# Products into one set of columns, ACT stores straight from the bank, and Pool on every second subtraction: one stage of a mixture-of-experts kernel on one core

## The chip, the core and the metric

One NeuronCore of a Trainium2 chip. TensorE (PE) multiplies into the eight banks of PSUM, VectorE (DVE) and ScalarE (ACT) read PSUM and SBUF, GpSimd (POOL) reads and writes SBUF here, SyncE (SP) issues the DMAs. The metric is the device time of one execution in microseconds (us); lower is better.

## What is computed

```python
X = np.fft.fft(np.fft.fft(x, axis=1), axis=2).real   # x: (8, 3072, 256)
x = X.reshape(24576, 256)
# eight groups of 3072 rows in the kernel: soft routing of rows to 32 slots and back
logits = x @ phi
slot_out = experts(softmax(logits, axis=0).T @ x)     # two small matmuls per expert
y = softmax(logits, axis=1) @ slot_out
# second mixture: three matmuls, a maximum, one matmul
h = np.maximum(np.maximum(y @ w1, y @ w2), y @ w3)
out = h @ w_out                                       # (24576, 768) @ (768, 256)
```

The softmax of the second line is over all rows of the input, so everything up to `slot_out` ends before any row of `out` can begin. That splits the kernel into two phases. The change is in the second.

## The kernel before

The first phase ends at about 207.7 us of the profiled execution. The second one (from `phase2`, L1095) makes the output. The slots are folded into the weights ahead of it, so that only a 64-row operand `ct` (the softmax over slots, split into a high and a low half) is multiplied: `gst` holds what takes `ct` to the hidden layer, `w_hl` the last weights.

The work is cut into 48 **blocks** of 512 columns (`blocks`, `NK` = 48), six to a group `b` of the input: `q` = 0, 1, 2, and two halves `h` of each `q`. The first group that is done is the last one of the input. A block has six **steps**, one for each 128 rows `f` of the hidden layer; `n` = 6k + f numbers the steps through. In step n each engine is given, in this order:

- PE: two matmuls of 512 columns, L983 and L984 (`pmm`), into two banks; there are two banks of either kind, so L984 of step n waits until DVE has read that of step n-2.
- ACT: `relu` of the first bank (L989, to `t`), then `high` (L999): the rounded copy `hi` of the hidden tile of step n-1.
- DVE: `low` (L1004): `lo` = h - hi of step n-2; then a piece of the next group's softmax; then `top` (L994): the maximum of the second bank and `t`.
- PE: the products of an earlier block with the last weights. For each f and each 128 columns j: `hi` times [w_hi, w_lo], 512 columns in one instruction (L1014), for f = 0 one of 256 columns with `ct` (L1018), then `lo` times w_hi, 256 columns (L1021). Four accumulators `o` of one bank each hold j = 0 to 3. One block has 24 x (512 + 256) + 4 x 256 = 19,456 columns of this kind and 6 x 1024 of the first.

Each engine works its instructions off in that order. For blocks 0 to 2 the products of index i = 6k + f stand `behind[i]` = 3 to 6 steps behind, for all four j at once (`omm_f`). From step 24 on (`ahead`) they stand in the order j, f: 6, 11 and 4 x 13 pieces in steps 24 to 29, then 76 pieces in every six steps, which is one block. In that order the piece of f = 5, j = 0 of block m is the last one of step 6(m+1)+1, and its `lo` is subtracted in that same step.

When an accumulator is full, `fin` makes the output of it: the sum stands in two halves, hi x w_hi + lo x w_hi in columns 0 to 255 and hi x w_lo in 256 to 511. ACT copies the bank to SBUF (L1040, `ab`), and Pool adds the halves into `osb` (L1043). For q = 0 and 2 this is one add on 128 partitions, for q = 1 two adds on 64, since the halves of the partitions go to different rows. In the last block ACT copies one half and DVE adds the other from the bank. When `osb` is full, SP stores it: one DMA (L1054), or one and eight small ones (L1061, L1063).

The softmax of the next group (`softmax2`) begins with a DMA of its logits on SP (L596, `tmp`) in steps 12, 36, 72 and so on, and its pieces follow one to a step on DVE, the first of them three steps later: L609 twice, L612 twice, L617 twice, L620, L623 twice, L627 twice, then eight steps of two transposes each (L634). Pool is given five of the subtractions L1004 (`pool_low`: steps 13, 15, 18, 20 and 22).

Of the kernel before, what the change touches and what calls it, by code (L numbers as in the profile page):

```python
# [7 lines left out]
F32 = mybir.dt.float32  # L8
# [4 lines left out]
ALU = mybir.AluOpType  # L13
# [140 lines left out]
def kernel(ctx: ExitStack, tc: tile.TileContext, x, phi, w1, w2, u1, u2, u3, wo,  # L154
                        t_f, t_ft, t_s2, t_s2t, t_cm, t_inv, t_id, out):
    nc = tc.nc
    NB = x.shape[0]
    NP, LAST = NB // 2, NB - 1
    mm, act, dve = nc.tensor.matmul, nc.scalar.activation, nc.vector
    COPY, RELU, EXP = ACTF.Copy, ACTF.Relu, ACTF.Exp  # L160
# [44 lines left out]
    def dma(cost, out, in_, r=(), w=(), behind=()):  # L205
        def go():
            o = out() if callable(out) else out
            nc.sync.dma_start(out=o, in_=in_)
        return add("SP", cost, go, r, w, behind=behind)
# [380 lines left out]
    ct_t = {}  # L590
# [90 lines left out]
    def table_f(g, behind):  # L681
        lo, hi = GR[g]
        return dma(182 * (hi - lo), f_sb[:, lo:hi], t_f[:, lo:hi], w=[f"f{g}"], behind=behind)

    load_x(0, 0)
    k = table_f(0, [xa_at[0, 0]])
    k = dma(182, phi_sb, phi.rearrange("(h p) s -> p h s", p=128), w=["phi"], behind=[k])
    k = dma(273, s2_sb, t_s2, w=["s2"], behind=[k])
    load_x(0, 1, [k])
    k = table_f(1, [xa_at[0, 1]])  # L690
    load_x(0, 2, [k])
    k = table_f(2, [xa_at[0, 2]])
    k = dma(1456, cm_sb, t_cm, w=["cm"], behind=[k])
    k = dma(182, ident, t_id, w=["id"], behind=[k])
# [3 lines left out]
    k = dma(273, s2t_sb, t_s2t, w=["s2t"], behind=[xa_at[1, 1]])  # L698
    dma(2367, ft_sb, t_ft, w=["ft"], behind=[xa_at[1, 2]])
    add("DVE", 500, consts, r=["id"], w=["rep"])  # L700
    for b in range(NB + 2):
# [32 lines left out]
        if b == 7:  # L734
# [22 lines left out]
            for i in range(2):  # L757
                for h in range(2):
                    add("POOL", 1820, lambda i=i, h=h: nc.gpsimd.tensor_tensor(out=u12[:, i, h], in0=u12[:, i, h], in1=u3_sb[:, h], op=ALU.subtract),
                        r=["u30", "u31", "u32"] + [f"u{1 + i}{t}" for t in range(3)], w=[f"d{i}{h}"])  # L760
# [123 lines left out]
    w_hl = wg[:, 0:3072].rearrange("p (c f) -> p c f", c=6)  # L884
    w_hi, w_lo = w_hl[:, :, 0:256], w_hl[:, :, 256:512]
    gst = wg[:, 3072:4864]
# [41 lines left out]
    for a in range(2):  # L928
        for h in range(2):
            for k in range(2 + a):  # L930
                for i in range(4):
                    n = (112, 80)[a] if k < 2 else 64
# [3 lines left out]
                       start=(h == 0 and k == 0), stop=(h == 1 and k == 1 + a))  # L936
        o = sm[a][:, 0:224]
# [4 lines left out]
    for a in range(2):  # L942
        n = (112, 80)[a]
        for j in range(2):
            o = sm[4 + 2 * a + j][:, 0:448].rearrange("p (i c) -> p i c", i=2)
# [3 lines left out]
            c = 448 * a + 2 * n * j  # L949
# [14 lines left out]
    dp3 = ctx.enter_context(tc.tile_pool(name="dp3", bufs=3, reuse_waits="tile"))  # L964
# [10 lines left out]
    NK = len(blocks)  # L975
# [32 lines left out]

    def products(k, f, j, o):

        b, q, h = blocks[k]
        hi, lo = hl[k, f]
        c = slice(128 * j, 128 * j + 128)
        mm(out=o, lhsT=hi[:, c], rhs=w_hl[:, f], start=(f == 0), stop=False)  # L1014
        yield
        yield
        if f == 0:
            mm(out=o[:, 0:256], lhsT=ct_t[b][:, q, 512 * h + 128 * j:512 * h + 128 * j + 128], rhs=gst[:, 1536:1792],  # L1018
               start=False, stop=False)
            yield  # L1020
        mm(out=o[:, 0:256], lhsT=lo[:, c], rhs=w_hi[:, f], start=False, stop=(f == 5))  # L1021
        yield

    def omm(k):

        for j in range(4):
            o = ps_o.tile([128, 512], F32, tag="o", name="o")
            for f in range(6):
                yield from products(k, f, j, o)
            late.append(lambda o=o, j=j: fin(k, 4 * blocks[k][2] + j, o))  # L1030

    def fin(k, i, o):

        b, q, h = blocks[k]
        if i == 0:
            o_sb[b, q] = dp3.tile([128, 8, 256], F32, tag="osb", name="osb")
        osb = o_sb[b, q]
        ab = dp3.tile([128, 512], F32, tag="ab", name="ab")
        last = k == NK - 1
        act(out=ab[:, 256 * last:512], in_=o[:, 256 * last:512], func=COPY)  # L1040
        for r, e in ((slice(0, (128, 64, 0)[q]), i), (slice((128, 64, 0)[q], 128), 7 - i)):
            if r.start < r.stop:
                (dve if last else nc.gpsimd).tensor_tensor(out=osb[r, e], in0=(o if last else ab)[r, 0:256],  # L1043
                                                           in1=ab[r, 256:512], op=ALU.add)
        if k >= NK - 2 and (last or i == 3):

            j = i if last else 0
            o_k = out[b * 3072:b * 3072 + 2048].rearrange("(k g j) d -> k g j d", g=16, j=8)[:, 0:8, j:i + 1]
            nc.sync.dma_start(out=o_k.rearrange("k g j d -> k g (j d)"), in_=osb[:, j:i + 1].rearrange("p j d -> p (j d)"))
        if i < 7 or last:  # L1050
            return
        o_k = out[b * 3072:(b + 1) * 3072].rearrange("(k r) d -> k r d", r=128)
        def plus(p0, k0, n):
            nc.sync.dma_start(  # L1054
                out=o_k[k0:k0 + n, 0:64].rearrange("k (g j) d -> k g (j d)", j=8),
                in_=osb[p0:p0 + 8 * n].rearrange("p j d -> p (j d)"))
        def minus(p0, k0, n):

            blk_ = o_k[k0:k0 + n]
            v = blk_[:, 64:128].rearrange("k (g j) d -> k g j d", j=8)[:, ::-1]  # L1060
            nc.sync.dma_start(out=v[:, :, 1:8], in_=osb[p0:p0 + 8 * n, 0:7])  # L1061
            for g in range(8):
                nc.sync.dma_start(out=blk_[:, 128 - 8 * g if g else 64], in_=osb[p0 + g:p0 + 8 * n:8, 7])  # L1063
        if q == 0:
            plus(0, 0, 16)
        elif q == 1:
            plus(0, 16, 8)
            minus(64, 0, 8)
        else:
            minus(0, 8, 16)  # L1070

    def omm_f(k, f):

        if f == 0:
            for j in range(4):
                o4[j] = ps_o.tile([128, 512], F32, tag="o", name="o")
        if k < len(behind) // 6 - 1 or f < 3:
            parts = [(f, j) for j in range(4)]
        else:

            parts = [(3 + i % 3, i // 3) for i in range(4 * f - 12, 4 * f - 8)]
        for f, j in parts:
            for _ in products(k, f, j, o4[j]):
                pass
            if f == 5:
                fin(k, 4 * blocks[k][2] + j, o4[j])
# [1 line left out]
    o4 = [None] * 4  # L1088
    late = []

    pool_low = (13, 15, 18, 20, 22)
    ahead = [6, 11, 13] + [13] * 3 + [13, 13, 13, 13, 12, 12] * NK
    behind = (3,) * 6 + (4,) * 3 + (5,) * 3 + (6,) * 6

# [123 lines left out]
```

## Time and profile before

| | |
|---|---|
| three runs | 783.50, 783.26, 777.71 us (median 783.26) |
| the profiled execution | 782.51 us, of which 780.7 us from the first to the last instruction |
| first phase, to the first L983 | 207.7 us |
| second phase, to the last matmul | 207.7 to 775.8 us |
| after the last matmul | 4.9 us: ACT copy, DVE add, DMA |

The two numbers of the profiled execution differ by 1.8 us, which lie outside its first and last instruction. "Busy" is the share of time in which an instruction of the engine was under way. Matmuls overlap: a row gives one of 512 columns as lasting 0.39 us, though the next one starts 0.23 us after it. So what PE loses is read from the starts, not from the busy time.

### The profile page before, as it was taken

The numbers are of one execution on the slowest core, as the hardware profiler recorded it, in microseconds if no ns is written. First come the engines' busy times: TensorE is split into PE (matmuls) and PEld (weight loads), VectorE is DVE, ScalarE is ACT, GpSimd is POOL, SyncE is SP. The second block draws the span as 40 slices with busy tenths as digits, with TensorE's granted clock in tenths as the row PEclk, the third lists the DMA queues.
The fourth block names the chain that finished last, engine by engine and source line by source line (L and its number), as shares of the span: only waits on it lengthen the run. The fifth ranks groups of instructions, "written<-read, shape, count | busy, mean of one in ns | idle before, by whom it ended". The sixth has DMA issues, their size and how long they took to land.

```text
span 780.7 us, 14128 instructions
## 1 busy us (share of the span) xinstructions
PE 742.5 (95%) x5324; PEld 613.2 (79%) x5324; DVE 570.9 (73%) x925; ACT 520.3 (67%) x974; POOL 302.8 (39%) x322
## 2 busy tenths in 40 slices
PE   5989898978999999999999999999999999999997
PEld 4557676675687778888888888888888888888886
DVE  2577575548579979769867976896698679766663
ACT  2356454434378677778777877877787777777773
POOL 4044543433028522533352344335333522533521
PEclk9999989999999999999999999999999999999999
DMA  9987877698402414322502251242225114312113
GB/s 347 407 316 275 286 235 249 202 291 276 97 1 55 111 46 96 94 74 54 133 10 69 56 134 52 62 98 55 75 55 135 30 45 95 95 55 55 29 36 99
DMA packets 37220, 97.26 MB, mean 125 GB/s; under 512 B 6048, under 2 KB 16672, under 8 KB 35744
## 3 DMA queue, kind: packets, MB, share of 16 engines
q1 hardware_dynamic: 33696, 83.78, 36.6%
q0 software_dynamic: 3456, 12.58, 4.5%
q8 instruction: 42, 0.69, 0.4%
q14 instruction: 26, 0.21, 0.1%
HBM read 55.44 MB, written 28.31 MB: 107 GB/s over the span
## 4 chain that ended last, share of the span: by engine, by line
PE 76%; DVE 9%; DMA 6%; ACT 3%; SPq 3%; issue 2%; POOL 1%; DVEq 0%; ACTq 0%; POOLq 0%
PE o L1014 30%; PE o L1021 16%; PE p L984 8%; PE p L983 7%; PE ap L318 4%; DMA xb<-in_x_dram,rev_sb 4%; PE o L1018 3%; SPq L1063 2%; PE zp L339 2%; PE vp L491 1%; DVE xf L266 1%; PE ap L474 1%; DVE h L994 1%; DVE d L461 1%; PE sm L902 1%
## 5 line engine op out<-in xcount | busy, mean ns | idle before, releaser
L1014 PE MATMUL o<-wg,hi 128*128 128x512 f32 x1152 | 424.3, 395 | 0.0
L1043 POOL TENSOR_TENSOR osb<-ab 64x256 f32<-64x256 f32 (+1 forms) x252 | 217.8, 865 | 353.0 <-ACT ab L1040 332.1
L1021 PE MATMUL o<-wg,lo 128*128 128x256 f32 x1152 | 323.3, 281 | 1.1 <-DVE lo L1004 1.0
L994 DVE TENSOR_TENSOR h<-p,t 128x512 f32<-128x512 f32 x288 | 196.8, 684 | 101.7 <-ACT t L989 100.9
L1014 PEld LDWEIGHTS o<-wg,hi 128*128 128x128 f32 x1152 | 216.1, 188 | 42.5
L989 ACT ACTIVATE t<-p 128x512 f32<-128x512 f32 x288 | 171.7, 597 | 99.9 <-PE p L983 99.5
L1021 PEld LDWEIGHTS o<-wg,lo 128*128 128x128 f32 x1152 | 216.8, 188 | 20.5 <-DVE lo L1004 3.5
L999 ACT ACTIVATE hi<-h 128x512 fp32r<-128x512 f32 x288 | 180.4, 626 | 32.0 <-DVE h L994 31.6
L1004 DVE TENSOR_TENSOR lo<-h,hi 128x512 fp32r<-128x512 f32 x283 | 200.3, 708 | 0.3 <-ACT hi L999 0.2
L984 PE MATMUL p<-ct,wg 128*128 128x512 f32 x288 | 115.1, 400 | 2.2 <-DVE h L994 2.1
L1040 ACT ACTIVATE ab<-o 128x512 f32<-128x512 f32 (+1 forms) x192 | 111.6, 584 | 7.0 <-PE o L1021 7.0
L983 PE MATMUL p<-ct,wg 128*128 128x512 f32 x288 | 113.9, 396 | 0.0
L318 PE MATMUL ap<-ff_sb,xf 128*128 128x128 f32 x416 | 58.0, 295 | 13.7 <-DVE xf L266 7.8
L318 PEld LDWEIGHTS ap<-ff_sb,xf 128*128 128x128 f32 x416 | 53.5, 206 | 17.6 <-DVE xf L266 8.4
L984 PEld LDWEIGHTS p<-ct,wg 128*128 128x128 f32 x288 | 54.2, 188 | 11.4 <-DVE h L994 7.7
L983 PEld LDWEIGHTS p<-ct,wg 128*128 128x128 f32 x288 | 54.2, 188 | 8.0 <-ACT t L989 0.4
L1018 PE MATMUL o<-wg,ct 128*128 128x256 f32 x192 | 53.6, 279 | 0.0
L324 ACT ACTIVATE a_sb<-ap 128x512 f32<-128x512 f32 (+1 forms) x56 | 31.0, 571 | 33.2 <-PE ap L318 33.1
L1018 PEld LDWEIGHTS o<-wg,ct 128*128 128x128 f32 x192 | 36.2, 188 | 4.1
L634 DVE STREAM_TRANSPOSE tmp<-tmp 96x256 f32<-96x256 f32 x56 | 30.5, 619 | 0.0
L339 PE MATMUL zp<-a_sb,pj_sb 128*32 128x512 f32 (+1 forms) x256 | 26.5, 546 | 3.4 <-ACT a_sb L324 3.0
L233 POOL DMA_INDIRECT xb<-in_x_dram,rev_sb x24 | 24.2, 1008 | 13.0 <-DVE xf L266 8.0
(163 smaller groups left out, 555.0 us busy)
## 6 DMA issues: line engine op xcount, KB each, us to landing
wu<-in_moe_w_dram SPq DMA_DIRECT2D x32, 512.0 KB
ct<-tmp SPq DMA_DIRECT2D x84, 128.0 KB
xf<-in_x_dram SPq DMA_DIRECT2D x16, 512.0 KB
out_dram<-osb SPq DMA_DIRECT2D x7, 1024.0 KB
out_dram<-osb SPq DMA_DIRECT2D x8, 896.0 KB
xf<-in_x_dram SPq DMA_DIRECT2D x8, 640.0 KB
raw<-in_moe_w_dram SPq DMA_DIRECT2D x9, 512.0 KB
out_dram<-osb SPq DMA_DIRECT2D x9, 512.0 KB
```

The lines of the kernel that those rows point to most:

```text
L318: mm(out=ap[:, c, j], lhsT=x_t[b][:, 2 * i + j, 128 * c:128 * c + 128], rhs=f_sb[:, 2 * i + j])
L983: mm(out=p1, lhsT=gst[:, 128 * f:128 * f + 128], rhs=ct)
L984: mm(out=p2, lhsT=gst[:, 768 + 128 * f:768 + 128 * f + 128], rhs=ct)
L989: act(out=t1, in_=p1, func=RELU)
L994: dve.tensor_tensor(out=h32, in0=p2, in1=t1, op=ALU.max)
L999: act(out=hi, in_=h32, func=COPY)
L1004: (nc.gpsimd if n in pool_low else dve).tensor_tensor(out=lo, in0=h32, in1=hi.bitcast(F32), op=ALU.subtract)
L1014: mm(out=o, lhsT=hi[:, c], rhs=w_hl[:, f], start=(f == 0), stop=False)
L1018: mm(out=o[:, 0:256], lhsT=ct_t[b][:, q, 512 * h + 128 * j:512 * h + 128 * j + 128], rhs=gst[:, 1536:1792], start=False, stop=False)
L1021: mm(out=o[:, 0:256], lhsT=lo[:, c], rhs=w_hi[:, f], start=False, stop=(f == 5))
L1040: act(out=ab[:, 256 * last:512], in_=o[:, 256 * last:512], func=COPY)
L1043: (dve if last else nc.gpsimd).tensor_tensor(out=osb[r, e], in0=(o if last else ab)[r, 0:256], in1=ab[r, 256:512], op=ALU.add)
```

## The change

For blocks 0 to 7 and block 47 (`whole`) the 512-column matmul becomes two of 256 columns, with w_hi and with w_lo, into the same 256 columns of the bank. The finished sum then stands there complete. `fin` stores it to `osb` with ACT straight from the bank, one instruction of 128 partitions or two of 64; in the last block ACT and DVE take turns (j = 0, 2 and 1, 3). No `ab` and no Pool add remain in these nine blocks. The subtractions L1004 of all odd steps from 7 to 47 (21 instead of 5) go to Pool. Blocks 8 to 46 are as before.

```diff
     def products(k, f, j, o):
...
-        mm(out=o, lhsT=hi[:, c], rhs=w_hl[:, f], start=(f == 0), stop=False)
-        yield
-        yield
+        u = o[:, 0:256]
+        if whole(k):
+            mm(out=u, lhsT=hi[:, c], rhs=w_hi[:, f], start=(f == 0), stop=False)
+            yield
+            mm(out=u, lhsT=hi[:, c], rhs=w_lo[:, f], start=False, stop=False)
+            yield
+        else:
+            mm(out=o, lhsT=hi[:, c], rhs=w_hl[:, f], start=(f == 0), stop=False)
+            yield
+            yield
...
+    def whole(k):
+        return k < 8 or k == NK - 1
...
-        ab = dp3.tile([128, 512], F32, tag="ab", name="ab")
         last = k == NK - 1
-        act(out=ab[:, 256 * last:512], in_=o[:, 256 * last:512], func=COPY)
-        for r, e in ((slice(0, (128, 64, 0)[q]), i), (slice((128, 64, 0)[q], 128), 7 - i)):
-            if r.start < r.stop:
-                (dve if last else nc.gpsimd).tensor_tensor(out=osb[r, e], in0=(o if last else ab)[r, 0:256],
-                                                           in1=ab[r, 256:512], op=ALU.add)
+        parts = [(r, e) for r, e in ((slice(0, (128, 64, 0)[q]), i), (slice((128, 64, 0)[q], 128), 7 - i))
+                 if r.start < r.stop]
+        if whole(k):
+            for r, e in parts:
+                if last and i % 2:
+                    dve.tensor_copy(out=osb[r, e], in_=o[r, 0:256])
+                else:
+                    act(out=osb[r, e], in_=o[r, 0:256], func=COPY)
+        else:
+            ab = dp3.tile([128, 512], F32, tag="ab", name="ab")
+            act(out=ab, in_=o, func=COPY)
+            for r, e in parts:
+                nc.gpsimd.tensor_tensor(out=osb[r, e], in0=ab[r, 0:256], in1=ab[r, 256:512], op=ALU.add)
...
-    pool_low = (13, 15, 18, 20, 22)
+    pool_low = [n for n in range(7, 48) if n % 2]
```

How the order moves, at three places. On **POOL**, from the end of the first phase on (`u_110` is a weight of that phase; `osb` the output tile, `h_` with a number the hidden tile of one step), before:

```order
L759 TENSOR_TENSOR u_110<-u_110,u3o 128x768 x2
L1043 TENSOR_TENSOR osb<-ab 128x256 x4
L1004 TENSOR_TENSOR lo<-h_2383,hi 128x512
L1004 TENSOR_TENSOR lo<-h_2427,hi 128x512
L1043 TENSOR_TENSOR osb<-ab 128x256 x4
L1004 TENSOR_TENSOR lo<-h_2483,hi 128x512
L1004 TENSOR_TENSOR lo<-h_2531,hi 128x512
L1043 TENSOR_TENSOR osb<-ab 64x256 x2
L1004 TENSOR_TENSOR lo<-h_2582,hi 128x512
L1043 TENSOR_TENSOR osb<-ab 64x256 x14
L1043 TENSOR_TENSOR osb<-ab 128x256 x16
```

and now, from the ninth subtraction to the first add:

```order
L1004 TENSOR_TENSOR lo<-h_2648,hi 128x512
L1004 TENSOR_TENSOR lo<-h_2704,hi 128x512
L1004 TENSOR_TENSOR lo<-h_2754,hi 128x512
L1004 TENSOR_TENSOR lo<-h_2809,hi 128x512
L1004 TENSOR_TENSOR lo<-h_2873,hi 128x512
L1004 TENSOR_TENSOR lo<-h_2945,hi 128x512
L1004 TENSOR_TENSOR lo<-h_2998,hi 128x512
L1004 TENSOR_TENSOR lo<-h_3049,hi 128x512
L1004 TENSOR_TENSOR lo<-h_3106,hi 128x512
L1004 TENSOR_TENSOR lo<-h_3161,hi 128x512
L1004 TENSOR_TENSOR lo<-h_3214,hi 128x512
L1062 TENSOR_TENSOR osb<-ab 64x256 x16
```

The 40 adds of blocks 0 to 7 are gone, and Pool has 21 subtractions with nothing between them, before the first add of block 8 (L1062).

On **DVE**, steps 24 to 27, where the softmax pieces L627 and L634 of the next group stand (`tmp`, `p_` and `t_` are its tile, a bank and a `relu` tile), before:

```order
L627 TENSOR_TENSOR tmp<-tmp 96x512
L994 TENSOR_TENSOR h_2686<-p_2675,t_2678 128x512
L1004 TENSOR_TENSOR lo<-h_2656,hi 128x512
L627 TENSOR_TENSOR tmp<-tmp 96x512
L994 TENSOR_TENSOR h_2704<-p_2694,t_2697 128x512
L1004 TENSOR_TENSOR lo<-h_2686,hi 128x512
L634 STREAM_TRANSPOSE tmp<-tmp 96x256 x2
L994 TENSOR_TENSOR h_2726<-p_2715,t_2718 128x512
L1004 TENSOR_TENSOR lo<-h_2704,hi 128x512
L634 STREAM_TRANSPOSE tmp<-tmp 96x256 x2
```

and now:

```order
L627 TENSOR_TENSOR tmp<-tmp 96x512
L994 TENSOR_TENSOR h_2704<-p_2693,t_2696 128x512
L627 TENSOR_TENSOR tmp<-tmp 96x512
L994 TENSOR_TENSOR h_2734<-p_2723,t_2726 128x512
L1004 TENSOR_TENSOR lo<-h_2704,hi 128x512
L634 STREAM_TRANSPOSE tmp<-tmp 96x256 x2
L994 TENSOR_TENSOR h_2754<-p_2744,t_2747 128x512
L634 STREAM_TRANSPOSE tmp<-tmp 96x256 x2
L994 TENSOR_TENSOR h_2809<-p_2796,t_2799 128x512
L1004 TENSOR_TENSOR lo<-h_2779,hi 128x512
```

Each second L1004 has left this engine's row.

On **DVE**, the end of the program, before:

```order
L1004 TENSOR_TENSOR lo<-h_9289,hi 128x512
L994 TENSOR_TENSOR h_9334<-p_9325,t_9328 128x512
L1004 TENSOR_TENSOR lo<-h_9314,hi 128x512
L1004 TENSOR_TENSOR lo<-h_9334,hi 128x512
L1043 TENSOR_TENSOR osb<-o,ab 128x256 x4
```

and now:

```order
L1004 TENSOR_TENSOR lo<-h_9417,hi 128x512
L994 TENSOR_TENSOR h_9462<-p_9453,t_9456 128x512
L1004 TENSOR_TENSOR lo<-h_9442,hi 128x512
L1004 TENSOR_TENSOR lo<-h_9462,hi 128x512
L1055 COPY osb<-o 128x256 x2
```

Four adds that each need a copy of ACT first become two copies from the bank; the other two tiles are ACT's. On PE, 216 matmuls with their weight loads are added (24 in each of nine blocks); the number of columns is the same.

## Rows read from the trace of the kernel before

**Rows 1.** Windows: length, busy us of PE, PEld, DVE, ACT, POOL (instructions), clock, DMA.

```profile
207.67:226.59 18.92, 18.70 (x98) 15.08 (x97) 14.07 (x24) 14.62 (x30) 2.93 (x4) 1.00 0.00 0
226.59:247.48 20.89, 20.46 (x110) 17.24 (x109) 19.29 (x30) 17.72 (x34) 12.68 (x11) 1.00 0.20 51
247.48:321.33 73.85, 71.81 (x381) 58.93 (x380) 64.96 (x105) 54.45 (x102) 33.77 (x35) 1.00 0.38 92
532.14:555.44 23.30, 23.30 (x129) 20.10 (x128) 15.63 (x25) 17.32 (x32) 11.04 (x15) 1.00 0.12 33
```

**Rows 2.** Timeline of PE: start, duration, instruction [idle before, releaser], steps 25 and 41.

```profile
248.64 0.40 PE L983 MATMUL p<-ct,wg 128*128 128x512 f32 x1
249.68 0.50 PE L984 MATMUL p<-ct,wg 128*128 128x512 f32 x1 [0.64 <-DVE h L994]
...
282.60 0.39 PE L983 MATMUL p<-ct,wg 128*128 128x512 f32 x1
283.62 0.50 PE L984 MATMUL p<-ct,wg 128*128 128x512 f32 x1 [0.63 <-DVE h L994]
```

**Rows 3.** Timeline of PE and of its weight loads, where 256-column or shorter matmuls follow each other.

```profile
401.79 0.27 PE L1018 MATMUL o<-wg,ct 128*128 128x256 f32 x1
401.90 0.28 PE L1021 MATMUL o<-wg,lo 128*128 128x256 f32 x1
402.02 0.40 PE L1014 MATMUL o<-wg,hi 128*128 128x512 f32 x1
...
205.90 1.64 PEld L948 LDWEIGHTS sm<-gt,pick 128*128 128x128 f32 x14 [0.21 <-DVE gt L939]
```

**Rows 4.** Timeline of DVE, three neighbouring instructions of the transposing steps.

```profile
253.64 0.68 DVE L994 TENSOR_TENSOR h<-p,t 128x512 f32<-128x512 f32 x1
254.24 0.68 DVE L1004 TENSOR_TENSOR lo<-h,hi 128x512 fp32r<-128x512 f32 x1
254.84 1.11 DVE L634 STREAM_TRANSPOSE tmp<-tmp 96x256 f32<-96x256 f32 x2
255.80 0.67 DVE L994 TENSOR_TENSOR h<-p,t 128x512 f32<-128x512 f32 x1
```

**Rows 5.** Timeline of POOL and DVE: a subtraction alone, one beside a softmax piece.

```profile
228.22 1.29 POOL L1004 TENSOR_TENSOR lo<-h,hi 128x512 fp32r<-128x512 f32 x1 [3.17 <-ACT hi L999]
...
246.85 1.63 POOL L1004 TENSOR_TENSOR lo<-h,hi 128x512 fp32r<-128x512 f32 x1
...
247.24 1.78 DVE L623 TENSOR_TENSOR tmp<-tmp,sm__2460 96x512 f32<-96x512 f32 x1
```

**Rows 6.** Groups of DVE, 226 to 312 us.

```profile
L623 DVE TENSOR_TENSOR tmp<-tmp,sm__3071 96x512 f32<-96x512 f32 x2 | 1.4, 678 | 0.0
```

**Rows 7.** Groups of ACT, 207 to 312 us and the last 16 us.

```profile
L1040 ACT ACTIVATE ab<-o 128x512 f32<-128x512 f32 x30 | 17.1, 590 | 0.0
...
L1040 ACT ACTIVATE ab<-o 128x256 f32<-128x256 f32 x4 | 1.5, 385 | 7.0 <-PE o L1021 7.0
```

**Rows 8.** Timelines of ACT, POOL, SP's queue and DVE, around the load for steps 39 on.

```profile
265.11 0.60 ACT L1040 ACTIVATE ab<-o 128x512 f32<-128x512 f32 x1
...
264.29 4.31 POOL L1043 TENSOR_TENSOR osb<-ab 64x256 f32<-64x256 f32 x4 [2.18 <-ACT ab L1040]
...
269.33 9.40 SPq L1063 DMA_DIRECT2D out_dram<-osb  x8
...
282.28 0.68 DVE L609 TENSOR_REDUCE mx<-tmp 96x16 f32<-96x512 f32 x1 [3.08 <-DMA tmp<-l_dram]
```

**Rows 9.** Timelines of ACT and PE, steps 36 and 37.

```profile
273.76 0.62 ACT L999 ACTIVATE hi<-h 128x512 fp32r<-128x512 f32 x1
...
276.68 0.28 PE L1021 MATMUL o<-wg,lo 128*128 128x256 f32 x1
```

**Rows 10.** Timeline of the last 5 us.

```profile
775.86 0.38 ACT L1040 ACTIVATE ab<-o 128x256 f32<-128x256 f32 x1 [1.75 <-PE o L1021]
776.28 0.42 DVE L1043 TENSOR_TENSOR osb<-o,ab 128x256 f32<-128x256 f32 x1 [1.72 <-ACT ab L1040]
```

More of the change, by code (lines that the diff above doesn't have):

```diff
@@ L1013, in products @@
         c = slice(128 * j, 128 * j + 128)
-        mm(out=o, lhsT=hi[:, c], rhs=w_hl[:, f], start=(f == 0), stop=False)
-        yield
-        yield
+        u = o[:, 0:256]
[8 more added lines that the diff above has]
+            yield
         if f == 0:
-            mm(out=o[:, 0:256], lhsT=ct_t[b][:, q, 512 * h + 128 * j:512 * h + 128 * j + 128], rhs=gst[:, 1536:1792],
+            mm(out=u, lhsT=ct_t[b][:, q, 512 * h + 128 * j:512 * h + 128 * j + 128], rhs=gst[:, 1536:1792],
                start=False, stop=False)
             yield
-        mm(out=o[:, 0:256], lhsT=lo[:, c], rhs=w_hi[:, f], start=False, stop=(f == 5))
+        mm(out=u, lhsT=lo[:, c], rhs=w_hi[:, f], start=False, stop=(f == 5))
         yield
+    def whole(k):
+        return k < 8 or k == NK - 1
     def omm(k):
```

## The prediction

> **What bounds the kernel now.** I read three views, in this order. First the windows of the second phase [rows 1]. The reader is to see its last row first: two regular blocks, 23.30 us, in which PE is busy for all 23.30 and DVE for 15.63. There PE is the bound, and as these two blocks have 2 x 25,600 = 51,200 columns, a column costs 0.455 ns. With that price the rows above it can be weighed. Steps 0 to 11 hold 12 x 1024 columns of L983 and L984 and eight of the products' indices, 26,624 columns: 38,912 in all, 17.7 us, and they last 18.92. Steps 12 to 23 hold 44,032, 20.0 us, and last 20.89. Steps 24 to 59 hold 36 x 1024 + 6 x 19,456 columns less the seven pieces (1,792 columns) by which the first of those blocks starts slower: 151,808, 69.1 us, and last 73.85. So PE loses 1.2, 0.85 and 4.75 us there, 6.8 us in all, and hardly anything afterwards in a block as those of the last row. This is the whole that a better balance in the first ten blocks can give back.
>
> Then the timeline of PE, for whom it waits [rows 2]. L983 and L984 should start 0.233 us apart (512 x 0.455). In step 25 they are 1.04 apart, in step 41 1.02, and both times the releaser is DVE's L994. DVE is the late engine; it was busy for 19.29 of 20.89 and for 64.96 of 73.85 us [rows 1].
>
> Last, why DVE is late. There are three reasons. (a) In the transposing steps its own queue is longer than a step: L994 and L1004 start 0.60 us apart, as do L1004 and the transposes, and two transposes take 0.96, so 2.16 us a step [rows 4] against 11.65 / 6 = 1.94. (b) It is stretched by Pool: a softmax piece L623 lasts 0.68 us alone [rows 6] and 1.78 beside a subtraction on Pool, which itself goes from 1.29 to 1.63 [rows 5]. (c) In steps 39 and 40 it stands still for 3.08 us for the logits of the next softmax, whose load waits on SP behind the stores of a tile (eight of them fill 9.40 us of its queue), and these behind Pool's adds [rows 8].
>
> **The change part by part.** *Two matmuls of 256 columns for one of 512* (216 more on PE, with as many weight loads). Where 256-column matmuls with different weights follow each other they start 0.11 and 0.12 us apart [rows 3], and two of 0.1165 (256 x 0.455) are one of 0.233. Three and more in a row are new. The nearest row is the one of 14 weight loads back to back, in 1.64 us to the end of the last one [rows 3]: 1.64 / 14 = 0.117 at most from one to the next, and less by what the last one's own duration takes of it. So a weight load hides under a matmul of 256 columns. I take nothing; the bounds are 0 and 216 x 0.01 = 2.2 us, 0.01 being the difference between the two distances in rows 3. That all three write the same columns is no new thing either: L1018 and L1021 do so in these rows. The Trainium skill (TensorE: Matmul & The Clock Gate, Back-to-back issue gap) speaks against the split, as it gives each matmul some 2.5 ns on top of its columns; by it the sum would be 216 x 2.5 ns = 0.5 us worse, an estimate from that page. The rows, at 0.01 us, can neither show nor exclude such a step.
>
> *Pool's 40 adds of blocks 0 to 7 go, 16 more subtractions come* (21 instead of 5). Pool is no bound on either side: 21 x 1.29 to 1.63 us [rows 5] is 27 to 34 us in 41 steps of 1.94. On DVE the 16 are worth 0.60 us each [rows 4], 9.6 us, where they were on its path: in steps 24 to 33 two steps now hold 2 x (0.60 + 0.96) + 0.60 = 3.7 us against 3.9. The queue no longer grows, where it grew by 0.2 us in each. With L627 in steps 24 and 25 the reason (b) remains, one subtraction of Pool beside them instead of a row of adds. PE's loss in blocks 4 and 5, most of the 4.75, should fall to some 0.6.
>
> *The stores to SBUF by ACT.* A copy of 512 columns is 0.590 us and one of 256 is 0.385 [rows 7]. The blocks with q = 0 and 2 (0, 1, 4 to 7) save 4 x 0.205 = 0.8 us of ACT each. Blocks 2 and 3 (q = 1) need two of 64 partitions in place of one copy; no such row is there, and the nearest is the one of 128 partitions with as many columns, 0.385, so 4 x 0.18 = 0.7 us more in each. ACT is busy for 17.72 of 20.89 us in steps 12 to 23 [rows 1], so this fits, though with little to spare. In the row behind these stores stand the next `relu` and `high`, for which DVE waits. I take 0; bounds 0 to 1.5 us.
>
> *What the earlier output does to SP.* The last copy of block 3 ends at 265.7 us, and the adds behind it at 268.6 [rows 8]. With ACT storing twice 0.385 from 265.1 on, the tile is complete at about 265.9. SP's stores and the load behind them move up by 2 us or a little more, and so does the landing at 282.28. DVE, which stood there for 3.08 us, then still waits for about 1 us, and L994 of step 41 is no longer late: its 0.8 us, and the lateness it leaves to the next steps, go. I put that at 1.4 us of the 4.75.
>
> *The subtraction of f = 5 on Pool.* In steps 31, 37 and 43 it is needed in the same step. `hi` is ready at 274.38 and PE uses the first of it at 276.68 [rows 9], 2.3 us later; Pool needs 1.29 to 1.63. It is in time, with 0.7 us or more to spare.
>
> *The last block.* A copy and an add of 0.42 end at 776.70, 0.84 us after the bank was ready [rows 10]. Now it is one DVE copy of 256 columns from the bank; no row has it, and I take the add's 0.42 (bounds 0.3 and 0.5). It saves 0.4 us, all of it at the end of the span.
>
> The sum: of 6.8 us the first 1.2 (the start of the pipeline, before the first moved subtraction can matter) stay. Of the other 5.6 I leave 1.2: 0.6 in blocks 4 and 5, 0.3 in blocks 2 and 3, and 0.3 for the rest. That is a gain of 4.4, with the tail 4.8 us. The profiled execution would take 782.5 - 4.8 = 777.7 us. The profiled execution lies 0.75 below the median of the runs, so on the median's scale 778.4.
>
> **The rivals.** *The stretch by Pool keeps DVE late* (A). Every second step has a subtraction on Pool, and if each of those beside a softmax piece stretches it as L623 was stretched, reason (b) eats most of (a). For it: rows 5. Against: Pool was busy for 46.5 us in steps 12 to 59 [rows 1] and will be for fewer, 18 x 1.29 to 1.63 plus some adds of block 8. Left is the gain through SP, 1.4, the tail, 0.4, and a part: 2 to 3 us, 780.3 to 781.3.
>
> *DVE becomes the bound by that stretch* (B), the other side. Price: 18 subtractions in steps 13 to 47, each stretching one instruction of DVE by 1.78 - 0.68 = 1.10, is 19.8 us; what DVE is rid of there is 13 x 0.60 = 7.8. Its 84.25 busy us in steps 12 to 59 [rows 1] would become 96.3, more than the 94.74 that they last, and the end would come 1.5 - 0.4 = 1.1 us later, at 784.4. It decides from a stretch of (94.74 - 84.25 + 7.8) / 18 = 1.02 us each. Against it: the 84.25 already hold the stretches by today's adds, and in every second step DVE has only L994, with one input from PSUM, beside the subtraction. The Trainium skill (SBUF — State Buffer, Who interferes with whom) has the rule behind this: a DVE instruction with two SBUF inputs and a Pool instruction that reads SBUF exclude each other, and the later one stands still until the other is done. By that rule Pool's whole duration could fall on DVE; rows 5 agree that both are lengthened, but for 0.3 us on Pool's side.
>
> *The change does not do on PE what it says* (C): a run of 256-column matmuls is slower than one of 512. If each extra one cost 0.05 us, an eighth of a matmul's duration, it would be 10.8 us less the 4.8: 789. Rows 3 speak against it.
>
> *All of it goes* (D): 5.6 + 0.4 = 6.0, or 7.2 with the start: 776.1 to 777.3. For it: regular blocks with a softmax in them lose next to nothing.
>
> **How the numbers follow.** My forecast (777.4 to 779.5) gets 0.60, A 0.20, D 0.11, B 0.06, C 0.03. One per cent is 7.8 us, about what a measurement of this kernel can tell from no change: the three runs alone lie 5.8 us apart. The trace offers 7.2 at most, so "faster by over 1%" takes the scatter of the runs on top of D or of the forecast: 0.12. "Slower by over 1%" needs C at a price above 0.06: 0.02. Within 1%: 0.86. The range goes up over A and most of the way to B, 783.0, and down to the lowest of the runs less the gain, 777.7 - 4.4 = 773.3, as the scatter seen before the change will be there after it.
>
> **What would show it.** In the profile after, L983 and L984 of steps 25 and 41 start 0.23 to 0.4 us apart; the steps 24 to 59 last 70 to 71 us, and 12 to 23 about 20.3; L1017, L1019 and L1029 of one f and j start 0.115 to 0.12 apart; L609 in steps 39 to 40 starts about 2 us earlier; the copy of the last bank ends 0.4 us after the last matmul. I am wrong if L994 still comes late behind an L623 or L627 of over 1.2 us (A, B), if PE waits for `lo` from Pool in steps 31, 37 or 43, if the 64-partition stores take longer than 0.4 us and hold up `relu`, or if the second phase is shorter by 5 us and the time is not, the first one having taken longer.

## The result and the profile after

The changed kernel takes 773.1 us (median of eleven runs, 771.07 to 777.36), the kernel before 780.92 beside it (776.16 to 783.50, which include the three runs shown above). The ratio is 0.9905, with a 95% interval of 0.9885 to 0.9924: faster by 5.9 to 9.0 us, within 1% at its middle. The profiled execution took 772.40 us, with a span of 770.5.

The windows of its second phase, cut at the same steps as [rows 1] (steps 0 to 11, 12 to 23, 24 to 59, and two regular blocks; busy us of PE, PEld, DVE, ACT, POOL, then clock and DMA):

```profile
203.16:222.22 19.06, 18.84 (x130) 16.76 (x129) 13.04 (x23) 13.98 (x30) 3.88 (x3) 1.00 0.00 1
222.22:242.50 20.28, 20.28 (x150) 19.22 (x149) 18.46 (x28) 16.91 (x35) 8.09 (x6) 1.00 0.21 53
242.50:313.21 70.71, 70.31 (x501) 65.72 (x500) 56.14 (x92) 52.68 (x108) 19.00 (x16) 1.00 0.39 96
523.18:546.48 23.30, 23.30 (x129) 20.11 (x128) 15.62 (x25) 17.32 (x32) 11.07 (x15) 1.00 0.12 33
```

PE is busy for all of steps 12 to 23, where it was short of that by 0.43 us, and is idle for 0.40 us in steps 24 to 59, where it was for 2.04. In steps 12 to 59 DVE has 9.65 us less to do (74.60 instead of 84.25), and Pool is busy for 27.09 us instead of 46.45. Two regular blocks last 23.30 us as before. The first ten blocks are shorter by 113.66 - 110.05 = 3.6 us.

The one long wait that is left, in the timelines of PE, POOL and ACT of the changed kernel (start, duration, instruction [idle before, releaser]):

```profile
246.12 0.28 PE L1019 MATMUL o<-wg,hi 128*128 128x256 f32 x1
246.80 0.38 PE L1029 MATMUL o<-wg,lo 128*128 128x256 f32 x1 [0.40 <-POOL lo L1004]
...
245.46 1.29 POOL L1004 TENSOR_TENSOR lo<-h,hi 128x512 fp32r<-128x512 f32 x1 [3.60 <-ACT hi L999]
...
242.70 1.54 ACT L1057 ACTIVATE osb<-o 64x256 f32<-64x256 f32 x4
244.26 0.60 ACT L989 ACTIVATE t<-p 128x512 f32<-128x512 f32 x1
244.76 0.62 ACT L999 ACTIVATE hi<-h 128x512 fp32r<-128x512 f32 x1
```

This is read from below: four stores of 64 partitions hold ACT for 1.54 us, `relu` starts at 244.26 for a bank that PE filled from 242.50 on, `hi` is ready at 245.38, and Pool's `lo` at 246.75. PE, which would have used it 0.12 us after 246.12, starts at 246.80. The subtraction is that of step 25, for f = 5 of block 3. PE needs its `lo` as the second piece of step 26: in steps 24 and 25 it has only 17 of the 19 pieces that block 3's j = 0 takes. So for block 3 this piece does not stand at the end of step 6(m+1)+1, as for the later blocks.

The groups of POOL and ACT from 203 to 307 us, and the last copy of the program:

```profile
L1004 POOL TENSOR_TENSOR lo<-h,hi 128x512 fp32r<-128x512 f32 x21 | 27.8, 1325 | 80.4 <-ACT hi L999 80.4
...
L1057 ACT ACTIVATE osb<-o 128x256 f32<-128x256 f32 x24 | 8.4, 380 | 0.0
L1057 ACT ACTIVATE osb<-o 64x256 f32<-64x256 f32 x16 | 6.0, 374 | 0.3 <-PE o L1029 0.2
...
766.48 0.42 DVE L1055 COPY osb<-o 128x256 f32<-128x256 f32 x1 [4.08 <-PE o L1029]
```

A subtraction on Pool takes 1.33 us on the mean, a store of 64 partitions as long as one of 128, and the copy of the last bank the 0.42 us of the add in [rows 10], without the ACT copy ahead of it. In a row, though, the two kinds of store differ: those of 128 partitions start 0.26 us apart, those of 64 partitions 0.37 to 0.39.

L983 and L984 of steps 25 and 41 start 0.23 us apart, as forecast. DVE's first softmax piece L609 of steps 36 on starts 8.44 us after the start of step 36, where it was 9.44 before, and DVE still stands still for 2.62 us ahead of it.

### The profile page after: what moved, and what is told of

Same layout as the page of the kernel before. It is cut to its first block, busy times and chain, and to the rows that moved or that the text cites. A ratio compares the mean times of both kernels' runs of the same rounds, so it can differ in the third digit from the quotient of the medians.

```text
span 770.5 us, 14517 instructions
## 1 busy us (share of the span) xinstructions
PE 738.5 (96%) x5540; PEld 624.2 (81%) x5540; DVE 558.2 (72%) x907; ACT 516.6 (67%) x980; POOL 287.0 (37%) x298
## 4 chain that ended last, share of the span: by engine, by line
PE 86%; DMA 5%; DVE 5%; ACT 2%; issue 1%; POOL 0%; SPq 0%; ACTq 0%; DVEq 0%; POOLq 0%
PE o L1022 28%; PE o L1029 18%; PE p L984 9%; PE p L983 8%; PE ap L318 3%; PE o L1017 3%; PE o L1019 3%; PE o L1026 3%; DMA xf<-in_x_dram 2%; PE zp L339 2%; PE vp L491 2%; DMA xb<-in_x_dram,rev_sb 2%; PE ap L474 1%; PE sm L902 1%; DMA raw<-in_moe_w_dram 1%
## 5 line engine op out<-in xcount | busy, mean ns | idle before, releaser
L1022 PE MATMUL o<-wg,hi 128*128 128x512 f32 x936 | 345.0, 395 | 0.0
L1062 POOL TENSOR_TENSOR osb<-ab 64x256 f32<-64x256 f32 (+1 forms) x212 | 180.6, 852 | 289.5 <-ACT ab L1060 266.8
L994 DVE TENSOR_TENSOR h<-p,t 128x512 f32<-128x512 f32 x288 | 196.9, 684 | 108.9 <-ACT t L989 106.3
L1004 DVE TENSOR_TENSOR lo<-h,hi 128x512 fp32r<-128x512 f32 x267 | 184.7, 692 | 0.3 <-ACT hi L999 0.2
L984 PE MATMUL p<-ct,wg 128*128 128x512 f32 x288 | 113.8, 395 | 0.2 <-DVE h L994 0.2
L983 PE MATMUL p<-ct,wg 128*128 128x512 f32 x288 | 113.9, 395 | 0.0
L1060 ACT ACTIVATE ab<-o 128x512 f32<-128x512 f32 x156 | 91.7, 588 | 0.0
L1017 PE MATMUL o<-wg,hi 128*128 128x256 f32 x216 | 60.8, 281 | 0.0
L1019 PE MATMUL o<-wg,hi 128*128 128x256 f32 x216 | 60.7, 281 | 0.0
L983 PEld LDWEIGHTS p<-ct,wg 128*128 128x128 f32 x288 | 54.3, 189 | 7.0 <-ACT t L989 0.4
L984 PEld LDWEIGHTS p<-ct,wg 128*128 128x128 f32 x288 | 54.4, 189 | 4.7 <-DVE h L994 0.8
L1004 POOL TENSOR_TENSOR lo<-h,hi 128x512 fp32r<-128x512 f32 x21 | 27.8, 1325 | 80.4 <-ACT hi L999 80.4
```

Source lines behind the costliest of these rows:

```text
L983: mm(out=p1, lhsT=gst[:, 128 * f:128 * f + 128], rhs=ct)
L984: mm(out=p2, lhsT=gst[:, 768 + 128 * f:768 + 128 * f + 128], rhs=ct)
L994: dve.tensor_tensor(out=h32, in0=p2, in1=t1, op=ALU.max)
L1004: (nc.gpsimd if n in pool_low else dve).tensor_tensor(out=lo, in0=h32, in1=hi.bitcast(F32), op=ALU.subtract)
L1017: mm(out=u, lhsT=hi[:, c], rhs=w_hi[:, f], start=(f == 0), stop=False)
L1060: act(out=ab, in_=o, func=COPY)
```

## What the profiles can tell apart

The second phase repeats well: one more profile of the kernel before and one of the changed kernel agree with the first ones within 0.4 and 0.1 us. The first phase does not. In the fourteen profiles of this study, whose first phase is the same code, it ends anywhere from 202.45 to 208.94 us. Effects of a microsecond are therefore read from the second phase, by its parts. All in us; "last" is the time from the start of the last matmul to the end of the span:

| kernel | ratio (95%) | phase 1 ends | phase 2 | steps 12-23 | 24-59 | blocks 10-47 | last |
|---|---|---|---|---|---|---|---|
| before | 1 | 207.67 | 573.05 | 20.89 | 73.85 | 454.21 | 5.18 |
| before again | - | 202.90 | 572.68 | 20.89 | 73.80 | 453.90 | 5.16 |
| changed | 0.9905 (0.9885-0.9924) | 203.16 | 567.32 | 20.28 | 70.71 | 452.95 | 4.31 |
| changed again | - | 204.78 | 567.41 | 20.28 | 70.72 | 453.02 | 4.32 |
| subtractions alone | 1.0197 (1.0162-1.0231) | 204.76 | 590.06 | 21.36 | 88.74 | 454.95 | 4.73 |
| stores alone | 0.9939 (0.9912-0.9965) | 203.26 | 567.63 | 20.28 | 71.04 | 452.92 | 4.32 |
| split everywhere | 1.0006 (0.9976-1.0036) | 204.12 | 577.10 | 21.02 | 73.88 | 457.95 | 5.17 |
| 64 more matmuls | - | 202.45 | 571.75 | 21.05 | 73.67 | 452.78 | 5.18 |
| 128 more | - | 203.97 | 572.28 | 21.04 | 73.32 | 453.67 | 5.17 |
| adds kept | - | 208.94 | 568.80 | 20.28 | 72.00 | 453.13 | 4.32 |
| without step 25 | 0.9925 (0.9894-0.9957) | 208.92 | 567.10 | 20.28 | 70.17 | 453.28 | 4.31 |
| last block alone | - | 206.12 | 572.85 | 20.89 | 73.81 | 454.45 | 4.75 |
| longer ACT | - | 207.23 | 567.58 | 20.28 | 70.71 | 453.19 | 4.32 |
| late store | - | 205.67 | 569.31 | 20.28 | 71.53 | 454.12 | 4.31 |

## The experiments

**Both kernels once more**, without an edit.

> The kernel before, once more, to see what moves without any change. If the first phase scatters, its end (207.7 us in the profile of before, 203.2 in the profile after, in the same code) lies anywhere from 203 to 208 here, and the rest of the span stays at 573.0 us within 1. If the later waits of before (blocks 19, 21, 37, 39, together 1.5 us) come by chance of the DMAs, they stand elsewhere or are fewer; if they belong to the kernel, they stand in the same blocks.

> The changed kernel, once more. Scatter of the first phase: its end lies anywhere from 203 to 208 us and the second phase again lasts 567.3 us within 1. If the change shortened the first phase itself, its end stays at 203 here while the kernel before stays at 207.

The end of the first phase was 202.90 for the kernel before, earlier than in the profile after, so it scatters and is no effect of the change that these profiles show. The second phase differs by 5.3 to 5.7 us. The later waits of before stand in blocks 19, 21 and 39 again (0.69, 0.35 and 0.34 us lost; 37 without), so they belong to the kernel for the most part.

**The subtractions alone:** the kernel before with

```diff
-    pool_low = (13, 15, 18, 20, 22)
+    pool_low = [n for n in range(7, 48) if n % 2]
```

> The kernel before with the 21 subtractions on Pool, adds and 512-column products as before. My theory (the gain needs both: Pool must be free of adds to take the subtractions): Pool has adds and subtractions in one row in blocks 2 and 3, PE waits for lo there, second phase 571 to 575 us, time within 0.3% of before. Rival 1 (relief of DVE alone does it): second phase 568 to 569, ratio 0.992 to 0.994.

My theory had the direction, but priced it far too low: 2% slower (1.6 to 2.3), 17 us more in the second phase. The timelines of POOL and PE of this kernel, in steps 25 and 26:

```profile
249.18 4.35 POOL L1043 TENSOR_TENSOR osb<-ab 64x256 f32<-64x256 f32 x4
253.61 1.27 POOL L1004 TENSOR_TENSOR lo<-h,hi 128x512 fp32r<-128x512 f32 x1
...
250.42 0.49 PE L984 MATMUL p<-ct,wg 128*128 128x512 f32 x1
254.94 0.58 PE L1021 MATMUL o<-wg,lo 128*128 128x256 f32 x1 [4.02 <-POOL lo L1004]
255.32 0.63 PE L1014 MATMUL o<-wg,hi 128*128 128x512 f32 x1
```

The subtraction stands behind four adds, and PE behind the subtraction. Six such waits make 13.6 us. Then comes what I had not counted. After 4 us without work PE's rows are spaced 0.43 us for 512 columns, and the windows show why (column 6 after the length is the granted clock):

```profile
250.00:254.70 4.70, 0.92 (x4) 0.22 (x2) 4.67 (x9) 2.15 (x4) 4.41 (x5) 0.95 0.00 2
254.70:260.40 5.70, 5.46 (x17) 4.69 (x18) 1.17 (x2) 1.60 (x3) 0.36 (x2) 0.50 0.61 135
```

The granted clock is 0.50, that is 1.2 GHz, for the next 5.7 us, so the wait is paid again in part by the work behind it. The second time it was so at 272 us, behind a wait of 3.3 us.

**The stores alone:** the changed kernel with the five old subtractions.

```diff
-    pool_low = [n for n in range(7, 48) if n % 2]
+    pool_low = (13, 15, 18, 20, 22)
```

> The changed kernel with the five old subtractions on Pool instead of 21. My theory: the load for the second softmax comes earlier and the tail is shorter, but DVE's row still grows by 0.2 us a step in the transposing steps: half of the gain, second phase 569.5 to 570.5 us, ratio 0.994 to 0.997. Rival 2 (the adds on Pool were the whole trouble, and the subtractions hardly matter): second phase 567 to 568.5, ratio 0.990 to 0.992.

The second phase is 567.63 us, 0.2 to 0.3 above the changed kernel. My theory falls here, and the second phase is that of rival 2: the new stores, without adds on Pool, bring nearly the whole gain. (The runs alone do not decide: their ratio, 0.9939, lies at the edge of my theory's range, and its interval overlaps that of the changed kernel.) The 16 more subtractions are worth 0.33 us in steps 24 to 59 and nothing elsewhere; and as the run "longer ACT" below, with the same five subtractions, lasts 70.71 us there like the changed kernel, not even this is shown to be theirs. DVE does every L1004 of steps 24 to 33 itself in the stores alone, and its row does grow there, by 0.1 us a step: L994 starts 3.07 us after its step's start in step 25 and 3.46 us in step 29. PE hardly waits for it, since it needs that bank only two steps later. In the kernel before, L994 was already 5.00 us behind in step 25: the lateness that PE felt came into these steps from the ones ahead of them.

**Split everywhere:** the kernel before with the product of f = 1 to 5 in two instructions, into the two halves of the bank.

```diff
-        mm(out=o, lhsT=hi[:, c], rhs=w_hl[:, f], start=(f == 0), stop=False)
-        yield
-        yield
+        if f:
+            mm(out=o[:, 0:256], lhsT=hi[:, c], rhs=w_hi[:, f], start=False, stop=False)
+            yield
+            mm(out=o[:, 256:512], lhsT=hi[:, c], rhs=w_lo[:, f], start=False, stop=False)
+            yield
+        else:
+            mm(out=o, lhsT=hi[:, c], rhs=w_hl[:, f], start=(f == 0), stop=False)
+            yield
+            yield
```

> The kernel before, with the 512-column product of f = 1 to 5 in all 48 blocks as two of 256 columns into the two halves of the bank: 960 matmuls and weight loads more, nothing else moved. My theory (a split costs nothing on PE): 256-column starts 0.115 to 0.12 us apart, second phase 573 us within 1.5, ratio 0.998 to 1.002. By 2.5 ns a matmul it would be 2.4 us more. Rival C of the prediction (0.05 us each): 48 us more, ratio 1.06.

The ratio is that of no change, but blocks 10 to 47 lasted 457.95 us against 452.78 in the kernel below, which has none of these splits there: 5.2 us for 38 x 20 = 760 of them, 6.8 ns each. In the timeline of PE:

```profile
499.94 0.28 PE L1015 MATMUL o<-wg,hi 128*128 128x256 f32 x1
500.06 0.28 PE L1017 MATMUL o<-wg,hi 128*128 128x256 f32 x1
500.18 0.28 PE L1027 MATMUL o<-wg,lo 128*128 128x256 f32 x1
500.30 0.28 PE L1015 MATMUL o<-wg,hi 128*128 128x256 f32 x1
```

In such a row each start is 0.119 us from the next on the mean, where 256 columns next to a matmul of 512 take 0.1165. So the split is not free: for the 216 of the change 1.5 us, inside my bounds of 0 to 2.2. Rival C is out by far. By the 2.5 ns of the Trainium skill (TensorE: Matmul & The Clock Gate, Back-to-back issue gap) it would be 0.5 us, an estimate from that page. The measured 6.8 ns decide.

**64 more and 128 more:** the same edit under a condition, so that only the first 64 or 128 matmuls are added, all ahead of block 8.

```diff
-        if f:
+        if f and (k < 3 or (k == 3 and f == 1)):      # 64
+        if f and (k < 6 or (k == 6 and f < 3)):       # 128
```

> The kernel before with only the first 64 of those splits (blocks 0 to 3). Theory on the later waits (blocks 19, 21, 37, 39 of before, gone in the changed kernel): a small store on SP takes 0.6 us longer when the 16 KB transfer of PE's next 128 matmuls falls on it, and the added matmuls move that transfer. 64 more is half a transfer, as the 192 of the changed kernel are one and a half: the waits vanish, blocks 10 to 47 take 452.9 to 453.1 us. Rival (the waits went because the output left earlier, or by the new order on Pool): they stay, 453.9 to 454.2.

> The same with the first 128 splits (blocks 0 to 6), one whole transfer: by the theory the transfers of the later blocks fall where they fell before, the waits are back in blocks 19, 21, 37 and 39, and blocks 10 to 47 take 453.9 to 454.2 us. If any change in the number of matmuls drives them away: 452.9 to 453.1.

These two ask why the changed kernel also lost the waits of blocks 19 to 39, whose code is as before. Three small stores of one tile in SP's queue, and the load of the next softmax behind them, in the kernel before; and the DMA queues in the window around the third:

```profile
416.96 2.41 SPq L1063 DMA_DIRECT2D out_dram<-osb  x3
419.41 0.44 SPq L596 DMA_DIRECT2D tmp<-l_dram  x1
...
q8 instruction: 1, 0.02, 3.0%
```

and the same three in the changed kernel, in whose window (409.0 to 411.0 us) no instruction transfer appears:

```profile
408.90 1.78 SPq L1081 DMA_DIRECT2D out_dram<-osb  x3
410.73 0.44 SPq L596 DMA_DIRECT2D tmp<-l_dram  x1
```

The transfers named "q8 instruction" are of 16 KB, one for each 128 matmuls or so, which is why I count them as PE's. With 64 more matmuls the waits are gone (452.78 us), with everything else of the kernel before in its place; so neither the earlier output nor the new order on Pool is needed for that. With 128 more, waits are back (453.67), though in blocks 31, 33 and 39, not where the theory had them. Before and with 128 more, one transfer of q8 falls into each of seven series of small stores, those of the tiles with q = 1 from block 8 on; in the changed kernel and with 64 more, none does. But a longer issue shows in only two of the seven in before, and in none with 128 more.

Two kinds of wait are to be told apart. The larger ones (0.45 to 0.7 us, in blocks 19, 31 and 37) stand behind a load for which DVE's L609 stood still for 2.0 to 2.6 us, against 0.9 to 1.7 for the other loads of these blocks, and they appear only in kernels that have such a transfer in these series. The smaller ones (0.35 us) do not need it: the late store below has as many matmuls as the changed kernel and no such transfer in these series, and yet it waits in blocks 15, 21, 33 and 39 (454.12 us), and without step 25 and longer ACT wait in block 39. So the place of the transfers goes with the larger waits only, and by which path they make a load late is open; what brings the smaller ones is open too.

**The adds kept:** the stores alone, and Pool still adds behind each of them, with nobody waiting for the result.

```diff
                 else:
                     act(out=osb[r, e], in_=o[r, 0:256], func=COPY)
+            if not last:
+                ab = dp3.tile([128, 512], F32, tag="ab", name="ab")
+                for r, e in parts:
+                    nc.gpsimd.tensor_tensor(out=ab[r, 0:256], in0=osb[r, e], in1=osb[r, e], op=ALU.add)
```

> The changed kernel with the five old subtractions on Pool, and with 40 adds left on Pool behind ACT's stores in blocks 0 to 7, for whose result nobody waits (they read the stored tile and write a scratch one; the output is the same). Theory (Pool's adds stretch DVE's two-input instructions, and that was the most of the loss): steps 12 to 59 take 93 to 94.7 us again, close to the 94.74 of before, against 91.3 without these adds, with L612, L623 and L627 over 1.2 us. Rival (the loss came through ACT's longer copies and the late load on SP, not through Pool's reads): 91.3 to 92 us.

Steps 12 to 59 took 92.28 us, against 91.32 without these adds: 1.0 of the 3.4 us that before lost more. That is nearer to the rival. (Pool is busy for 41.5 us there, in before for 46.5, in the stores alone for 9.6.) The groups of DVE in the first ten blocks, with the adds, and then without (stores alone):

```profile
L1004 DVE TENSOR_TENSOR lo<-h,hi 128x512 fp32r<-128x512 f32 x43 | 31.8, 738 | 0.0
L627 DVE TENSOR_TENSOR tmp<-tmp 96x512 f32<-96x512 f32 x4 | 3.5, 886 | 0.0
```

```profile
L1004 DVE TENSOR_TENSOR lo<-h,hi 128x512 fp32r<-128x512 f32 x43 | 29.1, 677 | 0.0
L627 DVE TENSOR_TENSOR tmp<-tmp 96x512 f32<-96x512 f32 x4 | 2.7, 680 | 0.0
```

The stretch is there, 9% on L1004 and 30% on L627, as the theory said; only it is not most of the loss. In steps 12 to 23 PE lost nothing by it. L994 of step 25 starts 3.74 us after its step's start, against 3.07 without the adds and 5.00 before: most of the lateness has another source.

**Longer ACT and late store:** the stores alone, each with one thing put back.

```diff
+            if not last and q != 1:
+                ab = dp3.tile([128, 512], F32, tag="ab", name="ab")
+                act(out=ab[:, 0:16], in_=o[:, 0:16], func=COPY)
```

```diff
+            if k == 3 and i > 5:
+                ab = dp3.tile([128, 512], F32, tag="ab", name="ab")
+                nc.gpsimd.memset(ab[:, 0:256], 0.0)
+                for r, e in parts:
+                    nc.gpsimd.tensor_tensor(out=osb[r, e], in0=osb[r, e], in1=ab[r, 0:256], op=ALU.add)
```

> The changed kernel with the five old subtractions, and with one more ACT copy of 16 columns behind each store of the blocks with q = 0 and 2 (24 small copies into a scratch tile, 0.2 us each by the distance of the 256- and 512-column copies), so that ACT spends there what it spent before the change. Theory (ACT's shorter copies are what is left: in block 3 of before DVE waited for relu, which stood behind four copies): steps 12 to 23 take 20.7 to 20.9 us instead of 20.28, steps 24 to 59 71.5 to 72.5 instead of 71.04. Rival (ACT has slack for it): 20.3 and 71.0 to 71.2.

> The changed kernel with the five old subtractions, and with Pool adding zeros to the last two pairs of tiles of block 3 ahead of SP's store, so that the store and the softmax load behind it leave some 3 us later, as before the change (the output stays the same). Theory (the late load costs PE in blocks 6 and 7): L609 of the second softmax starts 9.4 us after the start of step 36 instead of 8.9, the loss in blocks 6 and 7 goes from 0.95 to 1.5 us, steps 24 to 59 take 71.5 to 71.7 instead of 71.04. Rival (the load has slack): 71.0 to 71.2.

Longer ACT changes nothing (20.28 and 70.71 us), but it put back less than I meant. The copies or stores of block 1 and the `relu` of step 17 behind them, on ACT, in the kernel before, in the stores alone and in longer ACT:

```profile
234.10 2.14 ACT L1040 ACTIVATE ab<-o 128x512 f32<-128x512 f32 x4
236.13 0.59 ACT L989 ACTIVATE t<-p 128x512 f32<-128x512 f32 x1
...
229.90 1.20 ACT L1057 ACTIVATE osb<-o 128x256 f32<-128x256 f32 x4
230.96 0.63 ACT L989 ACTIVATE t<-p 128x512 f32<-128x512 f32 x1
...
233.88 0.38 ACT L1057 ACTIVATE osb<-o 128x256 f32<-128x256 f32 x1
234.14 0.19 ACT L1060 ACTIVATE ab<-o 128x16 f32<-128x16 f32 x1
234.21 0.40 ACT L1057 ACTIVATE osb<-o 128x256 f32<-128x256 f32 x1
...
235.19 0.68 ACT L989 ACTIVATE t<-p 128x512 f32<-128x512 f32 x1
```

From the first of them to `relu` it is 2.03 us before, 1.06 in the stores alone and 1.31 here: a copy of 16 columns lasts 0.2 us, but in such a row the next instruction starts 0.06 to 0.07 us after it. So the run put back a quarter of what the change took, and does not show that ACT's time is worth nothing. In before, `relu` of step 17 starts 1.0 us later after its step's start than in the stores alone, and DVE's L994 with it; ACT's longer copies remain a likely source of the rest, untested at their size.

The late load is worth 0.49 us against the stores alone, as expected, and 0.82 against longer ACT, which itself differs from the stores alone by 0.33: L609 starts 9.40 us after the start of step 36 instead of 8.90, and block 6 loses 0.86 us where it lost 0.36. In the timelines of DVE and PE of the late store:

```profile
277.74 0.68 DVE L609 TENSOR_REDUCE mx<-tmp 96x16 f32<-96x512 f32 x1 [2.97 <-DMA tmp<-l_dram]
278.34 0.68 DVE L994 TENSOR_TENSOR h<-p,t 128x512 f32<-128x512 f32 x1
...
278.25 0.39 PE L983 MATMUL p<-ct,wg 128*128 128x512 f32 x1
279.08 0.50 PE L984 MATMUL p<-ct,wg 128*128 128x512 f32 x1 [0.43 <-DVE h L994]
```

**Without step 25**, the changed kernel with that subtraction on DVE:

```diff
-    pool_low = [n for n in range(7, 48) if n % 2]
+    pool_low = [n for n in range(7, 48) if n % 2 and n != 25]
```

> The changed kernel with the subtraction of step 25 left on DVE (20 on Pool). Theory: the one wait of 0.56 us with its follower in block 4 goes, steps 24 to 59 take 70.0 to 70.2 us instead of 70.7, second phase 566.7. Rival (DVE, one subtraction more beside L627, is late in its turn): 70.5 to 71.

The wait is gone, 70.17 us instead of 70.71 in steps 24 to 59. It is the shortest second phase of all, 567.10, yet only by 0.2: a wait of 0.36 us stands in block 39 of this profile instead. The times do not part it from the changed kernel.

**The last block alone:** the kernel before with

```diff
+        return k == NK - 1
```

as `whole`.

> The kernel before with only the last block changed (24 splits, the store by ACT and DVE in turn). By the sum of the prediction the span behind the last matmul's start falls by 0.4 us, from 5.17 to 4.75. If the changed tail is worth all that the changed kernel shows there, it falls to 4.32. Everything ahead is as in before: steps 12 to 59 94.7 us.

4.75 us, to the hundredth the 0.42 us of the prediction. The other 0.43 that the changed kernel gains there comes with something else: the subtractions alone, with the last block of before, show 4.73. It lies behind the last DMA, in the closing instructions. In the six profiles that have it (both of before, split everywhere, 64 more, 128 more, the last block alone) POOL's closing DRAIN starts 0.36 us after the instruction ahead of it and takes 0.24 us, and a transfer of 8 KB on queue 14 (one more queue of instruction transfers) begins at the very end; in the others they are 0.07 and 0.10 us, and there is no such transfer. What sets it is open.

## Why the prediction came out as it did

The direction, the place and the lengths of the stretches were right; the largest term of the gain was put to the wrong part of the change. Steps 12 to 23 were to last about 20.3 us and last 20.28; steps 24 to 59 were to last 70 to 71 and last 70.71; the start of the pipeline kept its loss, 19.06 us for 18.92; the tail's copy gave its 0.42. The second phase was to shrink by 4.8 us and shrank by 5.3 to 5.7. The time itself, 773.1, lies 0.2 us under the low end of the range and 5.3 under the forecast. Term by term:

- *The reference.* The three runs had their median at 783.26, eleven have it at 780.92: 2.3 of the 5.3 us. I took the scatter of the runs into the range but not into the forecast, though the lowest of the three already lay 5.5 below.
- *"Hardly anything afterwards in a block."* Blocks 19, 21, 37 and 39 lost 1.8 us before and 0.3 in the changed kernel, which I had seen in no row since I read only two regular blocks. In blocks 10 to 47 the changed kernel got 0.9 to 1.3 us back, not by anything that the change is about: 64 added matmuls do the same, and the late store, with all of them, has lost it again.
- *The tail.* 0.85 us instead of 0.4; the other half is in the closing instructions, open.
- *The split taken at nothing.* It costs 6.8 ns each, 1.1 to 1.3 us for the 192 in blocks 0 to 7. It is why the gain in the first ten blocks is 3.6 us and not 4.4. [Rows 3] showed two distances in a row, and I took 0.11 and 0.12 for the same.
- *The 16 subtractions.* I let them cure the transposing steps, most of the gain. Measured: 0.3 us at most as they stand, and 0.5 to 0.9 with that of step 25 left on DVE (70.17 us against the 70.71 and 71.04 of the two kernels with five). What cured these steps is the new stores: they take the adds off Pool, shorten ACT's copies and let the load leave earlier. The sum came near because the stores gave what I had put to the subtractions, and that is luck. Reason (a), the row of DVE that grows in these steps, is real, but it is small and PE has room for it. Put back one at a time, the adds are worth 1.0 us and the late load 0.5, of 3.4 in all. The remaining 2.0 are not parted: the run with longer ACT put back a quarter of ACT's longer copies, and several things may act only together.
- *The load for the second softmax.* I let it come 2 us earlier, DVE wait for 1 us and the gain be 1.4 us. L609 came 1.0 us earlier and DVE still waited for 2.62, and the late load is worth 0.5 to 0.8 us.
- *The subtraction of f = 5.* I found it in time in steps 31, 37 and 43, and it is. In step 25, which I had left out, it is not: 0.56 us and 0.10 behind it, because of four 64-partition stores ahead of `relu`. That is the term of ACT's stores, which I set to 0 with a bound of 1.5 us; each takes 0.37 us, near the 0.385 that I took, but the four stand in one row.
- *Rivals.* A had the right mechanism and too high a price. The stretch by Pool is real (738 against 677 ns with the adds; beside a subtraction of the changed kernel an L623 takes 1.80 us and an L627 1.36), but PE did not wait for the L994 behind it. B and C are out: DVE's load fell by 9.65 us. D, with 7.2 us at most, was what the trace could give in the first ten blocks and the tail; the ratio's interval starts at 5.9.

The second phase accounts for 5.3 to 5.7 us, and the interval of the ratio for 5.9 to 9.0. The rest is not shown to be an effect: the end of the first phase moves by 6.5 us from profile to profile.

## What to carry to other kernels

When an engine is late, look for what stands in the same queue on the engines that feed it: the new stores, which take work off Pool and ACT, were worth more than the subtractions moved to Pool, and these without the stores cost 2%. A few profiles of the same kernel show which part of the time repeats; small effects should be read in that part, and the forecast be set against a median of more than three runs. An instruction that is split into two of half the size costs a little even where every column is the same, so split where another engine waits, and not everywhere. And what is put back to test a cause is to be measured in the trace: a short copy lasted 0.2 us, but held its engine for 0.06 to 0.07.

## What was not expected of the hardware

- A PE that waited for 4.0 us worked at 1.2 GHz for the next 5.7 us (granted clock 0.50), at 0.43 us for 512 columns instead of 0.233.
- Matmuls of 256 columns take 0.1165 us next to one of 512 and 0.119 in a row of their own.
- A store on ACT from 64 partitions takes as long as one from 128, 374 and 380 ns for 256 columns, and in a row it costs more: those of 64 partitions start 0.37 to 0.39 us apart, those of 128 overlap and start 0.26 us apart.
- How many matmuls stand ahead of a place moves when the transfers of q8 fall there. In the kernel before, each of seven series of small DMAs had one in it, in the changed kernel none, and an issue of 0.56 us took 1.19 in a series with one. Waits of 0.45 to 0.7 us in later blocks were seen only in kernels with such transfers; smaller ones were seen without them too.
